# Rows scattered whole into per-expert regions and read back by one plain DMA, with a finer routing plan

## The chip, the cores and the metric

The kernel runs on one core of a Trainium2 chip. The metric is the device time of one execution in microseconds (us). The engines are PE (TensorE, matmuls), DVE (VectorE), ACT (ScalarE), POOL (GpSimd) and SP (SyncE, here only a queue that issues DMAs).

## What is computed

A gated linear attention (hgrn2) over 4 batches, 8 heads, 768 positions and a head size of 48 gives 3072 rows of 384 values; a noisy top-2 router sends each row to 2 of 8 experts, a feed-forward of 384 to 1024 to 384 each, and the two results are added with softmax gates.

```python
for t in range(S):                                  # S = 768, B = 4, H = 8, D = 48
    state = f[:, :, t, :, None] * state + einsum('bhd,bhe->bhde', k[:, :, t], v[:, :, t])
    y[:, :, t] = einsum('bhd,bhde->bhe', q[:, :, t], state)
x = y.transpose(0, 2, 1, 3).reshape(B * S, H * D)   # 3072 rows of 384
noisy_logits = x @ w_gate + log1p(exp(x @ w_noise)) * noise
top2, top2_w = two largest of 8, their softmax
for e in range(8):
    for k in range(2):
        mask = top2[:, k] == e
        h = maximum(x[mask] @ w1[e], 0.0)           # 384 to 1024
        out[mask] += top2_w[mask, k, None] * (h @ w2[e])   # 1024 to 384
```

## The kernel before

**Attention.** Time is cut into 6 chunks of 128 positions. A unit of work is (chunk c, batch b), 24 in all. Two units run at once, their instructions interleaved step by step (two `stream`s): here such two units are called a pair, so there are 12 pairs, 0 to 11, two for each chunk. `prep` (L245) of a unit makes its decayed q and k two units ahead: transposes on PE (L254), a sigmoid on ACT, products and reciprocals on DVE. `main` (L287) makes near scores (L304), four levels of scores for distances 8, 16, 32 and 64 (`sc`, L326), each with masked copies into `scores` (DVE L341, the last level ACT L339) and decays of q and k between levels; the products named `aid` (L281, L307, L310, L330, L334) are on POOL for the first two chunks (`WIDE = 2`) and on DVE after. Then come `kx` (L349), the output `y` (L355, L360), the state `ds` (L371), and a transpose `xp` (L383) whose copy (L384) leaves the unit's 128 rows of 384 values in `xrow`.

**Routing.** After each chunk's four batches `route` (L390) makes logits (`lg`, L398), the top two, each row's gates, and by matmuls with ones and a triangle (`rk`, L424 to L429) each row's place in its expert's region; `ati` (L440) holds the places. The rows with their gates go from `xrow` into a DRAM table `xd` by four ACT DMAs (L446). POOL then issues eight indirect scatters (L452), one per batch and rank, each behind a short `memset` of `pause` (L451): they write *row numbers*, 4 bytes each, into `ids`, the table of expert regions. Last, `choose` (L463, on DVE) picks which full blocks of 128 rows may be worked on: `LIST[c]` of them, 9 after chunk 1, then 8, 8, 8, and 22 after the last chunk, 55 in all.

**Experts.** A block of 128 rows of one expert is loaded by `fetch_rows` (L501): SP reads the block's place from `row_no`, loads 128 row numbers (`places`, L504), and POOL gathers the rows from `xd` by them (`rows_in`, L509). The `places` load that comes next after a router waits for all eight of its scatters, whatever block it serves, since it is given those dependencies by hand:

```python
ins = nc.sync.dma_start(out=pl, in_=ids[bass.ds(at, C), :]).ins
for other in placed:
    tc.add_manual_dep(ins, other.name, ...)
placed.clear()
```

`fetch_weights` (L513) loads the expert's two matrices, 3.1 MB, by SP (L518) into one of two slots, unless that slot has this expert already. `block` (L547) transposes the rows (`bx`, L539), multiplies in two halves (`bh`, L562, 24 matmuls each, relu on ACT L565 into one buffer `h`), multiplies back (`by`, L573, 8 matmuls), scales by the gate (`yo`, ACT L577, two buffers) and has POOL add the 128 rows into the output by an indirect DMA (`out_dram<-yo`, L578), here called the accumulate. `bx` of the next block is issued ahead of `by` if its rows have been asked for. Rows are fetched three blocks ahead (four buffers), weights two.

**Order.** PE, like each engine, takes its instructions as they were issued. A block is six steps (`YIELDS = 6`); `fill` puts as many of them between the attention's steps as a goal asks for. No block runs before chunk 2; after its step 20 of 28 (its second pair) 5 blocks are spread to its end; chunks 3, 4, 5 end at 13, 21 and 29 blocks; the remaining 26, here called the tail, follow the last router.

## Time and profile before

| what | value |
|---|---|
| three runs | 1095.98, 1096.57, 1100.07 us; median 1096.57 |
| the profiled execution | 1099.49 us, span 1097.7 us |
| mean granted PE clock | 0.903 |
| busy, share of the span | PE 956.9 us (87%), PEld 776.4, DVE 413.9, ACT 241.0, POOL 276.6 |
| moved by DMA | 176.49 MB, mean 161 GB/s |

The span is from the first to the last instruction that the profiler saw in one execution; that execution's own time is 1.8 us longer. PEld is PE's loading of weights, which goes on beside its matmuls. The granted clock is the share of full TensorE speed that the chip allowed. A row of the timeline gives start, duration, engine, line, operation, output<-input, sizes, and in brackets the engine's idle time before it with what ended it. Pairs 0 and 1 end at 94.0 us of the span, pair 2 at 151.0, pair 3 at 185.0, pair 4 at 248.5 and pair 5, the end of chunk 2, at 336.4; the routers of chunks 2 to 5 begin at 336.4, 485.2, 634.7 and 774.8 us.

### The profile page before, as it was taken

What the parts mean: (1) busy time and instruction counts of PE and PEld (TensorE: products, weight loads), DVE (VectorE), ACT (ScalarE), POOL (GpSimd) and SP (SyncE); (2) the same over time, 40 slices, a digit from 0 to 9 for tenths busy, and PEclk for the clock granted to TensorE, in tenths of its full rate; (3) what the DMA queues carried; (4) which work ended last, traced back from release to release, by engine and by line L of the source; (5) the groups of instructions that cost most, each with busy time, mean ns of one, the idle gap of its engine ahead of it and who ended that gap; (6) DMA issues with size and microseconds to landing.
All of it is one profiled execution on the core that took longest, in us unless ns stands there. A gap on an engine that the chain in (4) does not pass through costs nothing. (4 is left out here: it accounts for less than half of the span.)

```text
span 1097.7 us, 18858 instructions
## 1 busy us (share of the span) xinstructions
PE 956.9 (87%) x7357; PEld 776.4 (71%) x7357; DVE 413.9 (38%) x1043; ACT 241.0 (22%) x494; POOL 276.6 (25%) x343
## 2 busy tenths in 40 slices
PE   3687587837999799999799997999949999999996
PEld 2566466726878577878578885787837878788775
DVE  5765565928314535527436364342300000000000
ACT  2233233112222222223113231212201111111111
POOL 2753541310113211203111141111312222222221
PEclk9887677566998899999899998999879999999999
DMA  9594214192762498663977665676738147153663
GB/s 139 133 317 73 29 31 59 32 286 44 222 197 59 133 251 259 141 192 98 302 230 227 202 177 194 209 245 203 216 122 267 31 128 249 28 148 101 187 199 73
DMA packets 188007, 176.49 MB, mean 161 GB/s; under 512 B 118272, under 2 KB 167585, under 8 KB 187920
## 3 DMA queue, kind: packets, MB, share of 16 engines
q1 hardware_dynamic: 71648, 132.49, 35.6%
q10 hardware_dynamic: 103296, 23.70, 13.1%
q0 software_dynamic: 12976, 19.12, 8.4%
q8 instruction: 58, 0.95, 0.4%
q14 instruction: 29, 0.24, 0.1%
HBM read 203.08 MB, written 25.30 MB: 208 GB/s over the span
## 5 line engine op out<-in xcount | busy, mean ns | idle before, releaser
L562 PEld LDWEIGHTS bh<-xT,w 128*128 128x128 f32 x2640 | 309.7, 194 | 19.5 <-issue 7.2
L562 PE MATMUL bh<-xT,w 128*128 128x128 f32 x2640 | 317.6, 278 | 4.4 <-issue 4.4
L573 PE MATMUL by<-w,h 128*128 128x384 f32 x880 | 310.1, 502 | 0.0
L573 PEld LDWEIGHTS by<-w,h 128*128 128x128 f32 x880 | 166.5, 197 | 103.4 <-issue 10.9
L578 POOL DMA_INDIRECT out_dram<-yo,places x55 | 88.2, 1603 | 333.4 <-ACT yo L577 331.6
L326 PE MATMUL sc<-fT,kQ 48*128 48x128 f32 (+1 forms) x1536 | 126.9, 314 | 32.6 <-DVE scores L341 10.9
L509 POOL DMA_INDIRECT rows_in<-xd,places x55 | 59.6, 1084 | 356.8 <-DMA places<-ids 198.2
L326 PEld LDWEIGHTS sc<-fT,kQ 48*128 48x128 f32 (+1 forms) x1536 | 107.3, 203 | 55.9 <-issue 18.3
L541 DVE COPY xT<-bx 128x384 f32<-128x384 f32 x55 | 30.6, 556 | 304.7 <-PE bx L539 304.5
L565 ACT ACTIVATE h<-bh 128x512 f32<-128x512 f32 x110 | 65.7, 597 | 238.6 <-PE bh L562 207.4
L577 ACT ACTIVATE yo<-by,gt 128x384 f32<-128x384 f32 x55 | 31.9, 580 | 250.8 <-PE by L573 243.1
L539 PE MATMUL bx<-ident,rows_in 128*128 128x128 f32 x165 | 29.4, 290 | 38.7 <-DMA rows_in<-xd,places 38.7
L452 POOL DMA_INDIRECT ids<-tokens,ati x48 | 48.6, 1013 | 50.9 <-DVE gt L443 43.3
L330 DVE TENSOR_TENSOR kQ<-kQ,T 128x256 f32<-128x256 f32 x60 | 25.3, 422 | 91.6 <-PE sc L326 88.5
L331 DVE TENSOR_TENSOR fT<-fT,T 128x256 f32<-128x256 f32 x96 | 41.5, 436 | 25.8 <-PE sc L326 17.5
L341 DVE COPY_PREDICATED scores<-masks,sc 128x512 f32<-128x512 uint8 x72 | 50.9, 707 | 0.0
L539 PEld LDWEIGHTS bx<-ident,rows_in 128*128 128x128 f32 x165 | 20.3, 148 | 40.9 <-issue 40.7
L363 DVE COPY yT<-y 48x512 f32<-48x512 f32 x16 | 11.1, 695 | 87.2 <-ACT yT L363 87.2
L355 PE MATMUL y<-scores,v 128*48 128x128 f32 x384 | 32.9, 326 | 12.5 <-ACT scores L339 12.5
L280 DVE RECIPROCAL back<-ahead 128x256 f32<-128x256 f32 x24 | 41.7, 1737 | 0.2
L282 DVE RECIPROCAL ahead<-back 128x256 f32<-128x256 f32 x24 | 41.5, 1727 | 0.0
L304 PE MATMUL near<-qT,kT 48*128 48x128 f32 x384 | 32.6, 321 | 7.1 <-DVE qT L283 7.1
(134 smaller groups left out, 810.3 us busy)
## 6 DMA issues: line engine op xcount, KB each, us to landing
w<-in_moe_w_dram SPq DMA_DIRECT2D x110, 1536.0 KB
xd<-zero SPq DMA_DIRECT2D x12, 392.0 KB
xd<-xrow ACTq DMA_DIRECT2D x24, 196.0 KB
f<-in_f_logit_dram ACTq DMA_DIRECT2D x24, 192.0 KB
q<-in_q_dram ACTq DMA_DIRECT2D x24, 192.0 KB
k<-in_k_dram ACTq DMA_DIRECT2D x24, 192.0 KB
v<-in_v_dram ACTq DMA_DIRECT2D x24, 192.0 KB
out_dram<-zero SPq DMA_DIRECT2D x12, 384.0 KB
```

The lines of the kernel that those rows point to most:

```text
L280: nc.vector.reciprocal(k8[:, :, 4:8], q8[:, :, 4:8])
L282: nc.vector.reciprocal(q8[:, :, 0:4], k8[:, :, 0:4])
L326: nc.tensor.matmul(sc[0:nj, par * HP + hp, :], lhsT=kQ[rows(par), hp * C:hp * C + nj], rhs=qP[rows(par), cols(hp)], start=True, stop=True)
L331: nc.vector.tensor_tensor(qv, qv, Tv[:, :, 0:1].broadcast_to((128, x, m)), ALU.mult)
L341: nc.vector.copy_predicated(Av, masks[:, l].rearrange("j (x m) -> j x m", m=m).unsqueeze(1).broadcast_to((C, H, nb, m)), scv)
L452: ins = nc.gpsimd.indirect_dma_start(out=ids, out_offset=bass.IndirectOffsetOnAxis(ap=ati[:, r, b:b + 1], axis=0), in_=tokens[:, c, b:b + ...
L509: nc.gpsimd.indirect_dma_start(out=xr, out_offset=None, in_=xd, in_offset=bass.IndirectOffsetOnAxis(ap=pl.bitcast(U32), axis=0), bounds_ch ...
L539: nc.tensor.transpose(p[:, j * 128:(j + 1) * 128], xr[:, j * 128:(j + 1) * 128], ident)
L562: nc.tensor.matmul(hp[:, f * 128:(f + 1) * 128], lhsT=w1[:, j, fo * 128:(fo + 1) * 128], rhs=xT[:, j * 128:(j + 1) * 128], start=(j == 0), ...
L565: nc.scalar.activation(h[:, half * 4:half * 4 + 4, :].rearrange("p f t -> p (f t)"), hp, AF.Relu)
L573: nc.tensor.matmul(yp, lhsT=h[:, fo, :], rhs=w2[:, fo, :], start=(fo == 0), stop=(fo == FO - 1))
L578: nc.gpsimd.indirect_dma_start(out=out, out_offset=bass.IndirectOffsetOnAxis(ap=pl, axis=0), in_=yo, in_offset=None, bounds_check=N - 1, o ...
```

## The change

**Whole rows are scattered.** A row is now 393 words: 384 values, 8 gates and its own number. `xd` and `ids` give way to one table `xs` with a region for each expert and one block of free rows (gate 0, a number out of range). `route` writes gates and number into `xrow` (POOL copies the number, after-line L435), and POOL's eight indirect scatters (after-line L471) write the rows to their places. A block's rows come by one plain SP DMA, `rows_in<-xs` (after-line L524); POOL's gather and the ACT DMAs into `xd` are gone. That DMA waits for scatters by the tracked overlap on `xs`, from which the scatters of routers later than the block's own list are excluded. After the last router eight plain POOL DMAs (after-lines L479 to L481) write 128 free rows behind the end of each region, where a region's last block is not full.

**The plan is finer.** There are seven routers: after chunk 0 (four batches), after each half of chunk 1, then after each chunk. Their lists have 1, 4, 4, 8, 8, 8 and 22 blocks. Goals are now set by pair, in blocks done at the end of pairs 0 to 11: 0, 0, 1, 2, 4, 6, 10, 13, 17, 21, 24, 28; the other 27 are the tail. For the first two routers the scatters go one by one between POOL's other steps; for all, `choose` comes ahead of them on DVE.

**Smaller edits.** The twelve DMAs that cleared `xd` and the memsets of `rows_in` are gone; `out` is cleared by one DMA in pair 1. The first two `prep`s copy k and q, and ask for the next loads, right behind the sigmoid.

The diff, cut to its core (other functions only take the group `i` and its `nb` batches for the chunk and `B`):

```diff
-    R = N
+    R = N + C
     XG = DM
-    XW = DM + E
+    XI = DM + E
+    XW = DM + E + 1
     BIG = 1 << 20
-    LIST = [0, 9, 8, 8, 8, 22]
+
+    GROUPS = [(0, 0, 4), (1, 0, 2), (1, 2, 2), (2, 0, 4), (3, 0, 4), (4, 0, 4), (5, 0, 4)]
+    LIST = [1, 4, 4, 8, 8, 8, 22]
+
+    GOALS = [0, 0, 1, 2, 4, 6, 10, 13, 17, 21, 24, 28]
...
-    xd = dram.tile([N, XW], F32, tag="xd", name="xd")
-    ids = dram.tile([NID, 1], I32, tag="ids", name="ids")
+    xs = dram.tile([E * R + C, XW], F32, tag="xs", name="xs")
     rows_in = [ctile([XW], f"rows_in{i}") for i in range(NR)]
-    places = [ctile([1], f"places{i}", I32) for i in range(NR)]
...
-        for t in rows_in + [zero, counts, used]:
+        for t in (zero, counts, used, free):
             nc.gpsimd.memset(t, 0.0)
+        nc.gpsimd.memset(free.bitcast(I32)[:, XI:XW], BIG)
         nc.gpsimd.memset(experts, -1.0)
-        nc.gpsimd.memset(free, BIG)
-        nc.sync.dma_start(out=ids.rearrange("(p r) o -> p (r o)", p=128), in_=free)
-        clear(xd, XW)
-
-    def clear(t, w):
-        for i in range(N // 128 // ZR):
-            nc.sync.dma_start(out=t[i * ZR * 128:(i + 1) * ZR * 128].rearrange("(p r) d -> p (r d)", p=128),
-                              in_=zero[:, 0:ZR * w])
+        nc.sync.dma_start(out=xs[E * R:E * R + C], in_=free)
+
+    def clear():
+        nc.sync.dma_start(out=out.rearrange("(l p) d -> p l d", p=128),
+                          in_=zero.unsqueeze(1).broadcast_to((128, N // 128, DM)))
...
-    def prep(c, b):
+    def prep(c, b, first=False):
...
+        def rest():
+            nc.scalar.copy(kT, transposed("k"))
+            nc.scalar.copy(qT, transposed("q"))
+            load(c * B + b + B)
+
         nc.scalar.activation(fT, transposed("f"), AF.Sigmoid)
+        if first:
+            rest()
...
-    def route(c):
+    def route(i):
+        c, b0, nb = GROUPS[i]
...
+        yTc, xr = yT[c % 2], xrow[c][:, b0:b0 + nb, :]
...
+        nc.gpsimd.tensor_copy(xr.bitcast(I32)[:, :, XI:XW], tokens[:, c, b0:b0 + nb].unsqueeze(2))
+        yield
...
+        nc.vector.tensor_tensor(xr[:, :, XG:XG + E], gt2[:, 0], gt2[:, 1], ALU.add)
...
-        nc.vector.tensor_tensor(counts, counts, rk[:, B], ALU.add)
-        nc.vector.tensor_tensor(base, base, rk[:, B], ALU.add)
-        nc.vector.tensor_tensor(gt2, hot, wide(ex), ALU.mult)
-        nc.vector.tensor_tensor(xrow[c][:, :, XG:XG + E], gt2[:, 0], gt2[:, 1], ALU.add)
-        for b in range(B):
-            nc.scalar.dma_start(out=xd[b * S + c * C:b * S + (c + 1) * C, :], in_=xrow[c][:, b, :])
+        nc.vector.tensor_tensor(base, base, rk[:, nb], ALU.add)
+        nc.vector.tensor_tensor(counts, counts, rk[:, nb], ALU.add)
+        if i == NG - 1:
+            nc.vector.tensor_copy(tails, base)
+        choose(i)
 
         mine = []
-        for b in range(B):
+
+        def put(ins):
+            for other in mine:
+                tc.declare_no_dep(ins, other, reason="distinct places")
+            mine.append(ins)
+            placed.append((i, ins))
+
+        for b in range(nb):
             for r in range(2):
                 nc.gpsimd.memset(pause, 0.0)
-                ins = nc.gpsimd.indirect_dma_start(
-                    out=ids, out_offset=bass.IndirectOffsetOnAxis(ap=ati[:, r, b:b + 1], axis=0),
-                    in_=tokens[:, c, b:b + 1], in_offset=None).ins
-                for other in mine:
-                    tc.declare_no_dep(ins, other, reason="distinct places")
-                mine.append(ins)
-        placed.extend(mine)
-        if LIST[c]:
-            choose(c)
-            ready[0] += LIST[c]
+                put(nc.gpsimd.indirect_dma_start(
+                    out=xs, out_offset=bass.IndirectOffsetOnAxis(ap=ati[:, r, b:b + 1], axis=0),
+                    in_=xr[:, b, :], in_offset=None).ins)
+                if i < 2:
+                    yield
+        if i == NG - 1:
+
+            for e in range(E):
+                at = nc.gpsimd.value_load(tails[0:1, e:e + 1], min_val=0, max_val=E * R)
+                nc.gpsimd.memset(pause, 0.0)
+                put(nc.gpsimd.dma_start(out=xs[bass.ds(at, C), :], in_=free).ins)
+        ready[0] += LIST[i]
...
-        nc.vector.tensor_scalar_mul(row_no[:, g:g + L], row, float(C))
+        nc.vector.tensor_scalar(row_no[:, g:g + L], row, float(C), float(E * R), ALU.mult, ALU.min)
...
-        xr, pl = rows_in[g % NR], places[g % NR]
-        at = nc.sync.value_load(row_no[0:1, g:g + 1], min_val=0, max_val=NID - C)
-        ins = nc.sync.dma_start(out=pl, in_=ids[bass.ds(at, C), :]).ins
-        for other in placed:
-            tc.add_manual_dep(ins, other.name, mybir.DependencyInfo(mybir.DependencyClass.Sync,
-                                                                    mybir.DependencyReason.DATA), reason="all places")
-        placed.clear()
-        nc.gpsimd.indirect_dma_start(
-            out=xr, out_offset=None, in_=xd,
-            in_offset=bass.IndirectOffsetOnAxis(ap=pl.bitcast(U32), axis=0), bounds_check=N - 1, oob_is_err=False)
+        at = nc.sync.value_load(row_no[0:1, g:g + 1], min_val=0, max_val=E * R)
+        ins = nc.sync.dma_start(out=rows_in[g % NR], in_=xs[bass.ds(at, C), :]).ins
+
+        for i, other in placed:
+            if i > listed[g][0]:
+                tc.declare_no_dep(ins, other, reason="distinct places")
...
-        pl = places[g % NR].bitcast(U32)
+        ids = rows_in[g % NR].bitcast(U32)[:, XI:XW]
...
-    def stream(c, first):
-
-        for b in (first, first + 2):
-            n = c * B + b + 2
-            p = prep(*order[n]) if n < len(order) else iter(())
-            for i, _ in enumerate(main(c, b)):
-                if i in (1, 3):
-                    next(p, None)
-                yield
-
-    TURNS = B * (len(LEVELS) + 3)
+    def stream(n):
+
+        p = prep(*order[n + 2]) if n + 2 < len(order) else iter(())
+        for i, _ in enumerate(main(*order[n])):
+            if i in (1, 3):
+                next(p, None)
+            yield
+
+    TURNS = 2 * (len(LEVELS) + 3)
...
+            for _ in prep(*order[n], first=True):
...
-        for c in range(NCH):
-            xrow[c] = wk.tile([128, B, XW], F32, tag="xrow", name=f"xrow{c}", bufs=2)
-
-            first = 20 if c == WIDE else 0
-            start = done[0]
-            goal = YIELDS * max(0, sum(LIST[:c]) - KEEP)
+        for pair in range(len(order) // 2):
+            if pair % 2 == 0:
+                c = pair // 2
+                xrow[c] = wk.tile([128, B, XW], F32, tag="xrow", name=f"xrow{c}", bufs=2)
+            start, goal = done[0], YIELDS * GOALS[pair]
             t = 0
-            streams = [stream(c, 0), stream(c, 1)]
+            streams = [stream(2 * pair), stream(2 * pair + 1)]
             while streams:
                 for x in list(streams):
                     turn()
...
                         streams.remove(x)
                         continue
                     t += 1
-                    if c >= WIDE:
-                        fill(start + (goal - start) * max(0, t - first) // (TURNS - first))
-                if c == 0 and t == 4:
+                    fill(start + (goal - start) * t // TURNS)
+                if t == 4 and pair == 0:
                     later_constants()
-                if c == 1 and t == 4:
-                    clear(out, DM)
-            assert router is None
-            router = route(c)
-        while router:
+                if t == 4 and pair == 1:
+                    clear()
+            c, b0, nb = GROUPS[group]
+            if c * B + b0 + nb == 2 * pair + 2:
+                routers.append(route(group))
+                group += 1
```

**Where it moves instructions.** In these rows `places_157` to `places_160` and `rows_in_153` to `rows_in_156` are the four buffers in turn, `DMASW..` is a lane of POOL's DMAs, `DMAHW..` one of SP's and ACT's, and `w_0`, `w_1` are the two weight slots.

SP's queue before, from the row load of block 6 (first row) to that of block 8 (last row), both of the list made after chunk 1:

```order
L504 DMA places_159<-ids 128x1 [waits DMAHW1_49,DMASW7_49,DMASW2_49]
L514 TENSOR_LOAD load_no
...
L518 DMA w_0_161<-in_moe_w_dram 128x3x1024 [waits DMAHW2_49,PE_49]
...
L503 TENSOR_LOAD row_no
L503 ISA x2
L504 REGISTER_ALU
L504 DMA places_160<-ids 128x1 [waits DMASW5_49,DMASW4_49,DMASW6_49,DMASW3_49,DMASW7_49,DMASW2_49,DMAHW0_49,DMASW1_49,DMASW0_49]
...
L518 DMA w_1_162<-in_moe_w_dram 128x3x1024 [waits DMAHW6_49,DMAHW1_49,PE_49]
...
L504 DMA places_157<-ids 128x1 [waits DMAHW3_49]
```

The `places` load of block 7 stands behind all eight POOL lanes, that is behind every scatter of chunk 2, and the weights of the next block stand behind it.

SP's queue in the change, from the row load of block 7 (first row) to that of block 9 (last row), the first block of the list made after chunk 2:

```order
L524 DMA rows_in_156<-xs 128x393 [waits DMAHW3_49,DMAHW7_49,DMASW3_49,DVE_49]
L531 TENSOR_LOAD load_no
...
L535 DMA w_1_158<-in_moe_w_dram 128x3x1024 [waits DMAHW6_49,DMAHW0_49,PE_49]
...
L524 DMA rows_in_153<-xs 128x393 [waits DMAHW0_49,DMASW4_49,DVE_49]
...
L535 DMA w_0_157<-in_moe_w_dram 128x3x1024 [waits DMAHW4_49,DMAHW1_49,PE_49]
...
L523 TENSOR_LOAD row_no [waits DVE_49]
L523 ISA x2
L524 ISA
L524 DMA rows_in_154<-xs 128x393 [waits DMAHW3_49,DMASW5_49,DMAHW5_49,DMASW4_49,DVE_49]
```

Blocks 7 and 8 wait on one POOL lane each, that of the accumulate that read their buffer's row numbers; block 9 waits on two, the accumulate's and that of the eighth scatter.

PE in pair 2 (chunk 1, batches 0 and 1) before, from the last level's scores on:

```order
L326 MATMUL sc_1_0_1200<-fT_0_661,kQ_0_951 64x128 x8
L326 MATMUL sc_1_1_1214<-fT_1_696,kQ_1_1009 64x128 x8
L349 MATMUL kx_0_1228<-ident,kQ_0_951 128x128 x4
L355 MATMUL y_0_1234<-scores_113,v_0_596 48x128 x8
L360 MATMUL y_0_1234<-fT_0_661,st_0_588 48x128 x8
```

The same place in the change:

```order
L334 MATMUL sc_1_0_1197<-fT_0_646,kQ_0_944 64x128 x8
L334 MATMUL sc_1_1_1211<-fT_1_681,kQ_1_1004 64x128 x8
L556 MATMUL bx_1246<-ident,rows_in_153 128x128 x3
L579 MATMUL bh_0_1257<-xT_1250,w_0_157 128x128 x12
L579 MATMUL bh_0_1271<-xT_1250,w_0_157 128x128 x6
L357 MATMUL kx_0_1278<-ident,kQ_0_944 128x128 x4
L363 MATMUL y_0_1284<-scores_113,v_0_581 48x128 x8
```

Block 0 is now between the scores and `kx`: the attention behind it on PE goes on when block 0's rows and the weights of its first halves are there.

POOL after the last chunk, before:

```order
L578 DMA out_dram<-yo_6676,places_157 3072x384
L451 MEMSET pause 128x1
L452 DMA ids<-tokens,ati_6696 27392x1
...
L509 DMA rows_in_156<-xd,places_160 128x392
L578 DMA out_dram<-yo_6822,places_158 3072x384
```

And in the change, down to the accumulate of block 27 (last row):

```order
L435 COPY xrow_5427<-tokens 128x4
L470 MEMSET pause 128x1
L471 DMA xs<-xrow_5427,ati_6567 25728x393
...
L479 TENSOR_LOAD tails
L479 ISA x2
L480 MEMSET pause 128x1
L481 ISA
L481 DMA xs<-free 128x393
...
L595 DMA out_dram<-yo_6710,rows_in_156 3072x384
```

Where the gather and the accumulate followed eight scatters, one accumulate now follows eight scatters and eight writes of free rows, each with its register load and memset.

## Rows read from the trace of the kernel before

**Rows 1.** The page: busy time, share of the span and instructions of each engine.

```profile
PE 956.9 (87%) x7357; PEld 776.4 (71%) x7357; DVE 413.9 (38%) x1043; ACT 241.0 (22%) x494; POOL 276.6 (25%) x343
```

**Rows 2.** Stretches: us, busy PE, PEld, DVE, ACT, POOL; PE clock, DMA share, GB/s.

```profile
94.00:151.00 57.00, 40.43 (x342) 35.06 (x340) 26.52 (x61) 14.42 (x32) 26.80 (x42) 0.61 0.23 43
151.00:185.00 34.00, 27.18 (x299) 22.45 (x298) 23.60 (x38) 11.45 (x26) 8.67 (x17) 0.80 0.34 48
185.00:248.50 63.50, 40.18 (x343) 34.47 (x342) 35.91 (x104) 13.40 (x30) 12.55 (x18) 0.60 0.54 146
248.50:336.40 87.90, 81.13 (x627) 67.20 (x627) 35.02 (x82) 19.02 (x39) 10.59 (x8) 0.88 0.55 150
336.40:774.80 438.40, 416.12 (x3413) 333.10 (x3412) 203.72 (x539) 104.12 (x214) 92.69 (x96) 0.96 0.66 199
774.80:1097.70 322.90, 295.29 (x1792) 237.26 (x1790) 27.19 (x118) 50.02 (x85) 77.67 (x68) 0.96 0.48 142
```

**Rows 3.** Timeline of PE: the waits for rows after each router.

```profile
380.40 0.88 PE L539 MATMUL bx<-ident,rows_in 128*128 128x128 f32 x3 [6.42 <-DMA rows_in<-xd,places]
...
529.12 0.87 PE L539 MATMUL bx<-ident,rows_in 128*128 128x128 f32 x3 [7.95 <-DMA rows_in<-xd,places]
...
677.10 0.87 PE L539 MATMUL bx<-ident,rows_in 128*128 128x128 f32 x3 [7.15 <-DMA rows_in<-xd,places]
...
820.22 0.87 PE L539 MATMUL bx<-ident,rows_in 128*128 128x128 f32 x3 [16.08 <-DMA rows_in<-xd,places]
820.88 7.06 PE L573 MATMUL by<-w,h 128*128 128x384 f32 x16
```

**Rows 4.** Timeline of POOL: scatters after chunk 2 (first) and chunk 5 (first, eighth).

```profile
350.00 1.00 POOL L452 DMA_INDIRECT ids<-tokens,ati  x1 [0.19 <-DVE whole L474]
...
786.84 0.97 POOL L452 DMA_INDIRECT ids<-tokens,ati  x1 [3.12 <-DVE gt L443]
...
795.70 0.95 POOL L452 DMA_INDIRECT ids<-tokens,ati  x1 [0.19 <-issue]
```

**Rows 5.** Timeline of SP's queue: the first `places` load after those scatters.

```profile
370.86 0.34 SPq L504 DMA_DIRECT2D places<-ids  x1
...
811.12 0.35 SPq L504 DMA_DIRECT2D places<-ids  x1
```

**Rows 6.** Timeline of PE: one block of the tail.

```profile
849.47 5.52 PE L562 MATMUL bh<-xT,w 128*128 128x128 f32 x48
854.83 0.49 PE L539 MATMUL bx<-ident,rows_in 128*128 128x128 f32 x3
855.15 5.33 PE L573 MATMUL by<-w,h 128*128 128x384 f32 x16
860.32 5.52 PE L562 MATMUL bh<-xT,w 128*128 128x128 f32 x48
```

**Rows 7.** Timeline of PE: idle gaps in pairs 2 and 4.

```profile
118.40 2.08 PE L326 MATMUL sc<-fT,kQ 48*128 48x128 f32 x16 [8.54 <-POOL fT L307]
...
226.02 1.08 PE L349 MATMUL kx<-ident,kQ 128*128 128x128 f32 x4 [4.36 <-DVE kQ L330]
239.29 1.95 PE L355 MATMUL y<-scores,v 128*48 128x128 f32 x16 [12.19 <-ACT scores L339]
```

**Rows 8.** Timeline of SP's and ACT's queues: first weights, and loads held behind them.

```profile
222.10 1.16 SPq L518 DMA_DIRECT2D w<-in_moe_w_dram  x2
...
229.64 0.37 ACTq L220 DMA_DIRECT2D f<-in_f_logit_dram  x1
234.49 0.37 ACTq L220 DMA_DIRECT2D q<-in_q_dram  x1
```

**Rows 9.** Timeline of POOL: an accumulate and the gather that waited for it.

```profile
393.19 1.76 POOL L578 DMA_INDIRECT out_dram<-yo,places  x1 [4.43 <-ACT yo L577]
401.32 1.05 POOL L509 DMA_INDIRECT rows_in<-xd,places  x1 [6.37 <-DMA out_dram<-yo,places]
```

**Rows 10.** Timeline of DVE: its first work after the last router.

```profile
821.12 0.56 DVE L541 COPY xT<-bx 128x384 f32<-128x384 f32 x1 [26.64 <-PE bx L539]
```

More of the change, by code (lines that the diff above doesn't have):

```diff
@@ L81 @@
     NR = 4
-    KEEP = 4
     WIDE = 2
     assert (H * D, 2 * LEVELS[-1], B * S, FO, B) == (DM, C, N, 8, 4)
-    assert all(sum(LIST[:c + 1]) <= max(0, 2 * B * (c + 1) - E + 1) for c in range(NCH - 1))
+    assert all(sum(LIST[:i + 1]) <= 2 * sum(nb for _, _, nb in GROUPS[:i + 1]) - E + 1 for i in range(NG - 1))
     assert NB == 2 * N // C + E - 1
@@ L148 @@
     base = ctile([E], "base")
-    i_no = {L: ctile([L], f"i_no{L}") for L in sorted(set(LIST)) if L}
+    i_no = {L: ctile([L], f"i_no{L}") for L in sorted(set(LIST))}
     tokens = ctile([NCH, B], "tokens", I32)
@@ L166 @@
     row_no = ctile([NB], "row_no", I32)
-    picks = [ctile([LIST[c], E], f"picks{c}") if LIST[c] else None for c in range(NCH)]
-    ZR = 2
-    zero = ctile([ZR * XW], "zero")
-    free = ctile([NID // 128], "free", I32)
+    picks = [ctile([LIST[i], E], f"picks{i}") for i in range(NG)]
+    zero = ctile([DM], "zero")
+    free = ctile([XW], "free")
+    tails = ctile([E], "tails", I32)
     def iota(t, pattern, mult, first=0):
@@ L276, in prep @@
         yield
-        nc.scalar.copy(kT, transposed("k"))
-        nc.scalar.copy(qT, transposed("q"))
-        load(c * B + b + B)
+        if not first:
+            rest()
         nc.vector.reciprocal(k8[:, :, 4:8], q8[:, :, 4:8])
@@ new lines, in route @@
+        nc.tensor.matmul(rk[:, 1:nb + 1], lhsT=ones, rhs=chosen[:, 0:1].broadcast_to((128, nb, E)), start=True,
+                         stop=False, skip_group_check=True)
+        nc.tensor.matmul(rk[:, 0], lhsT=before, rhs=chosen[:, 0], start=False, stop=True, skip_group_check=True)
+        nc.tensor.matmul(rk[:, 1:nb], lhsT=before, rhs=chosen[:, 1:nb], start=False, stop=False, skip_group_check=True)
+        for b in range(1, nb):
+            nc.tensor.matmul(rk[:, b + 1:nb + 1], lhsT=ones, rhs=chosen[:, b:b + 1].broadcast_to((128, nb - b, E)),
+                             start=False, stop=(b == nb - 1), skip_group_check=True)
@@ L518, in fetch_weights @@
             nc.sync.dma_start(out=w, in_=src, bounds_check="skip_entire_dma", cond=go)
-    listed = [(c, i) for c in range(NCH) for i in range(LIST[c])]
+    listed = [(c, i) for c in range(NG) for i in range(LIST[c])]
     ready, rows_done, weights_done = [0], [0], [0]
@@ L578, in block @@
         nc.gpsimd.indirect_dma_start(
-            out=out, out_offset=bass.IndirectOffsetOnAxis(ap=pl, axis=0), in_=yo, in_offset=None,
+            out=out, out_offset=bass.IndirectOffsetOnAxis(ap=ids, axis=0), in_=yo, in_offset=None,
             bounds_check=N - 1, oob_is_err=False, compute_op=ALU.add)
@@ L616 @@
         for n in range(2):
-            for _ in prep(*order[n]):
+            for _ in prep(*order[n], first=True):
                 pass
-        router = None
+        routers = []
+        group = 0
         def turn():
-            nonlocal router
-            if router and next(router, True):
-                router = None
-        for c in range(NCH):
-            xrow[c] = wk.tile([128, B, XW], F32, tag="xrow", name=f"xrow{c}", bufs=2)
-            first = 20 if c == WIDE else 0
-            start = done[0]
-            goal = YIELDS * max(0, sum(LIST[:c]) - KEEP)
+            if routers and next(routers[0], True):
+                routers.pop(0)
+        for pair in range(len(order) // 2):
[3 more added lines that the diff above has]
+            start, goal = done[0], YIELDS * GOALS[pair]
             t = 0
-            streams = [stream(c, 0), stream(c, 1)]
+            streams = [stream(2 * pair), stream(2 * pair + 1)]
             while streams:
```

54 lines of the change are left out of this document (24 added, 30 removed).

## The prediction

> **What bounds the kernel now.** I read the page first, then the busy time by stretch, then the PE timeline's idle gaps, then the queues that end them.
>
> The page: PE is busy 956.9 us of the 1097.7, so 140.8 us are idle [rows 1]. By stretch [rows 2]: from 336.4 us (end of chunk 2) to the end PE is busy 416.1 + 295.3 of 761.3 us at a granted clock of 0.96, almost PE-bound; from 94.0 to 248.5 us (pairs 2, 3, 4) it is busy 107.8 of 154.5 us at 0.60 to 0.80, a chain of DVE, POOL, ACT and small matmuls with no expert block beside it; 248.5 to 336.4 us holds the first 4.75 blocks.
>
> So time can come from two places: PE's gaps in the PE-bound part, and filling the early part with blocks. In the PE-bound part the gaps are few and named: 6.42, 7.95, 7.15 and 16.08 us before a `bx`, all ended by the rows' DMA [rows 3]. What is late there: after a router POOL issues eight scatters of row numbers, the first at 350.00 us [rows 4], and SP's next `places` load goes out only at 370.86 us [rows 5], when all eight have landed, 20.9 us after the first issue; after the last router 786.84 to 811.12 us, 24.3 us. The rows that PE waits for at 380.40 us are those of block 7, which is in the *old* list; the order (section on the change) shows its `places` load held by eight POOL lanes although only blocks from 9 on need the new scatters.
>
> **The change, part by part.** The sum is made against the profiled execution, span 1097.7 us. A block in the tail costs 10.85 us of PE, from one bh to the next (849.47 to 860.32 us) [rows 6].
>
> *1. Old lists no longer wait (336.4 to 774.8 us).* Row loads are plain SP DMAs, and in the order block 7's row load waits only for its buffer. Only block 9 and on waits for the new scatters, and block 9 is needed in the middle of block 8, some 45 us after the router starts (2.5 blocks at a quarter of a 68 us pair each, plus the router's own matmuls); landed scatters: about 34 us after it (336.4 to 370.86). So 6.42 + 7.95 + 7.15 = 21.5 us go. Behind such a gap PE runs cold: bx 0.87 for 0.49 and by 7.06 for 5.33 us [rows 3, 6], 2.1 us each, 6.3 more. Gain 27.8, bounds 15 (if block 9 is late by one such gap of half size at each router) and 27.8. The goals also do 22 blocks here for 24: -21.7 us of work. 438.4 - 27.8 - 21.7 = 388.9.
>
> *2. The tail (774.8 us to the end).* It has 27 blocks, not 26: +10.85. Five listed blocks are left at the last router, not four, and none waits for scatters, so the 16.08 us wait on rows goes. What is late next: POOL now issues eight row scatters, then eight plain DMAs for the tails, each behind a register load and a memset, and only then block 27's accumulate into out. ACT's `yo` of block 29 needs that buffer (two buffers), and block 30's h stands behind it on ACT. The eight scatters are issued by 795.70 + 0.96 = 796.7 us, 1.27 us apart [rows 4]. A tail write is unknown: 1.27 us like a scatter below, 3.0 above (the 24.3 us in which eight landed, by eight). I take 2.2, for the register load comes on top of a scatter's issue: the accumulate goes out at 814 us, takes 1.6 and lands 6.4 us later (393.19 + 1.76 to 401.32) [rows 9], 822; a queue still landing scatters until 811 pushes it to about 826. PE gets to block 30's by near 815 us and needs two ACT steps after the landing: wait about 12 us, bounds 0 and 25 (seventeen landings at 3.0). 322.9 + 10.85 - (16.1 - 12) = 329.7.
>
> Here one rule bears. DVE has nothing to do for 26.64 us before 821.12 us [rows 10], yet these are the slowest eight scatters of the run, 24.3 us against 20.9 beside a busy DVE [rows 4, 5]. The Trainium skill (SBUF — State Buffer, "SBUF: two separate sides") says that DMAs issued from GpSimd starve for descriptors while DVE holds the shared port; by that rule the tail, with DVE idle, would land at once and the sum would be 12 us lower. The trace disagrees, and the row decides.
>
> *3. Pairs 2 and 3 (94.0 to 185.0 us).* Today 57.0 + 34.0 = 91.0 us [rows 2]. Removed: the second stream's POOL steps no longer stand behind all eight scatters, 8.54 us of PE [rows 7]; the scatters now go one by one between POOL's steps, 1.27 us each [rows 4], covered by cold matmuls (if not covered, 10 us come back). Added: 1.75 blocks, 19.0 us. And two waits: PE's block 0 stands behind the last level's matmuls, and its rows need the eighth scatter, then SP loads rows, then weights. A landing of 2.6 us (20.9 by eight) and 7.5 us from the weights' issue to the end of their first half (222.10 to 229.64) [rows 8] make 10; bounds 5 and 20. Block 1 waits in pair 3 for its four scatters with block 0's accumulate between them: 7 us, bounds 0 and 12.4 (both halves, to 234.49) [rows 8]. 91.0 - 8.5 + 19.0 + 17 = 118.5.
>
> *4. Pairs 4 and 5 (185.0 to 336.4 us).* Today 151.4 us with 4.75 blocks. ACT stood at its loads' issue until the first weights had landed (229.64 and 234.49 us, [rows 8]), which left PE idle 4.36 + 12.19 us [rows 7]; the first weights come two pairs earlier, so this moves into term 3. Four blocks are left here. Above: 151.4 - 16.6 - 0.75 x 10.85 = 126.7. Below: as full as the later pairs, (438.4 - 27.8 - 24 x 10.85)/6 = 25.0 us of attention, (25.0 + 21.7) x 2 = 93.4. Pair 5's own attention beside its blocks, 87.9 - 4.75 x 10.85 = 36.4 [rows 2], lies between; I take the middle, 110.
>
> *5. Edits at nothing.* The 12 DMAs that cleared xd, the four 0.4 us memsets of rows_in and the POOL gathers (1.06 us each) go, `choose` moves ahead of the scatters on DVE, the first two preps copy k and q before the small copies: all beside the startup's loads or a PE that is the bound; if the cover is gone, 1 or 2 us either way.
>
> Sum: 94.0 + 118.5 + 110 + 388.9 + 329.7 = 1041.1 us of span. The profiled execution took 1.8 us more than its span and 2.9 us more than the median of the three runs (1099.49 to 1096.57), so **1040 us** as such a median, 5.2% less. The mechanism's own range: 12 and 16.7 us in the early part, 12 at the tail, up to 13 at the routers: 1015 to 1070.
>
> **Rivals.**
> *A, slower: scatters of whole rows land one by one.* Today's scatters carry 4 bytes a row; an accumulate, which carries whole rows, lands 6.4 us after its issue [rows 9]. If each row scatter occupies the queue that long, eight take 51 us. Block 9 is then 22 us late and the two later lists 6 each; pair 2 waits 24 more, pair 3 19, the tail (17 landings) 70: 147 us, 1187. It turns slower than before where it costs more than 57 us, at some 4.3 us a landing. Against it: the gathers of whole rows are issued at a scatter's price and PE's steady tail lives with one gather and one accumulate per block.
> *B, the early blocks are not hidden.* Waits of 20 and 12.4 us and pairs 4 and 5 at 126.7: 32 us more, 1072. For it: PE takes instructions in order, so a late row load holds the attention chain too; and ACT's loads share semaphores with SP's, which is what held it at 221 us today.
> *C, everything fits.* Waits of 5 and 0, pairs 4 and 5 at 93.4, no wait in the tail: 41 us less, 999. For it: from 336.4 us on pairs with four blocks do run full [rows 2].
> *D, the change doesn't do what it says:* old lists still wait, through another lane. Term 1's 27.8 us stay: 1068. Against it stands the order.
>
> **How the numbers follow.** Forecast 0.63, A 0.07, B 0.14, C 0.11, D 0.05. About half a per cent, 5.5 us, is what a measurement of this kernel tells from no change. Only A, or B beyond its bounds, comes near the old time: slower 0.06, same 0.03, faster 0.91. The range leaves out A, part of C and the top of B: 1008 to 1072.
>
> **What would show it.** Right: no `bx` after 350 us waits for its rows; SP issues the row loads of a list's last blocks before the newest scatters land; PE's wait in the tail is on ACT's h or yo, ended by an accumulate's landing; two waits of 5 to 20 us at the first two blocks; the end of chunk 2 near 322 us, with one block more done. Wrong: gaps of 6 us or more after each router still ended by the rows' DMA (D or A), a span from 94 to the end of chunk 2 over 260 us (B), or scatters that take more than 4 us each from the first issue to the last landing (A).

## The result and the profile after

The change takes 1040.8 us (median of 4 runs) beside 1098.2 us for the kernel before: 0.948 of its time, 95% interval 0.944 to 0.952. The forecast was 1040. The profiled execution took 1043.8 us, span 1042.2 us, mean granted clock 0.936.

Busy time by stretch, columns as in [rows 2]; the stretches are the start (pairs 0 and 1), pair 2, pair 3, pair 4, pair 5, the rest to the last router, and the tail:

```profile
0.00:102.54 102.54, 61.36 (x553) 51.74 (x554) 62.65 (x102) 28.62 (x68) 46.54 (x94) 0.90 0.68 119
102.54:171.38 68.84, 46.61 (x401) 40.71 (x400) 38.27 (x82) 16.31 (x35) 23.30 (x41) 0.68 0.38 102
171.38:229.91 58.53, 43.75 (x381) 37.13 (x379) 32.18 (x78) 15.19 (x34) 15.76 (x29) 0.74 0.55 160
229.91:282.00 52.09, 48.55 (x426) 38.74 (x424) 36.71 (x104) 16.40 (x35) 7.48 (x9) 0.90 0.63 179
282.00:329.48 47.48, 46.67 (x464) 37.83 (x463) 32.06 (x69) 14.12 (x31) 3.33 (x4) 1.00 0.72 188
329.48:722.11 392.63, 389.49 (x3281) 314.50 (x3280) 200.47 (x533) 99.29 (x208) 62.40 (x73) 0.98 0.72 217
722.11:1042.20 320.09, 307.04 (x1871) 245.50 (x1869) 28.82 (x125) 52.31 (x89) 57.21 (x59) 0.98 0.55 168
```

| term of the sum | forecast | measured | off by |
|---|---|---|---|
| start | 94.0 | 102.5 | +8.5 |
| pairs 2, 3 (term 3) | 118.5 | 127.4 | +8.9 |
| pairs 4, 5 (term 4) | 110 | 99.6 | -10.4 |
| to the last router (term 1) | 388.9 | 392.6 | +3.7 |
| tail (term 2) | 329.7 | 320.1 | -9.6 |
| span | 1041.1 | 1042.2 | +1.1 |

Every term is off by 4 to 10 us and the sum by 1: that the errors cancel is luck, so the experiments go to the terms.

**Start.** Timeline of PE and of ACT with its DMA queue, end of pair 0:

```profile
65.77 1.95 PE L363 MATMUL y<-scores,v 128*48 128x128 f32 x16 [6.87 <-ACT scores L347]
```

```profile
52.11 3.53 ACTq L221 DMA_DIRECT2D k<-in_k_dram  x1
55.68 0.59 ACT L265 COPY kT<-kp 128x512 f32<-128x512 f32 x1 [5.26 <-PE sc L334]
55.73 5.24 ACTq L221 DMA_DIRECT2D f<-in_f_logit_dram  x1
...
61.01 3.14 ACTq L221 DMA_DIRECT2D q<-in_q_dram  x1
...
65.14 1.06 ACT L347 COPY scores<-sc 64x512 f32<-64x512 f32 x2 [8.38 <-issue]
```

ACT stands 3 to 5 us at the issue of single loads, it copies the scores only after 8.38 us without other work, and PE's `y` waits for that. SP issued the one DMA that clears the output, 4.6 MB, at 47.05 us.

**The first two blocks.** Timeline of PE in pairs 2 and 3:

```profile
147.72 0.87 PE L556 MATMUL bx<-ident,rows_in 128*128 128x128 f32 x3 [7.52 <-DMA rows_in<-xs]
153.45 6.54 PE L579 MATMUL bh<-xT,w 128*128 128x128 f32 x36 [4.86 <-DMA w<-in_moe_w_dram]
...
177.07 0.58 PE L440 MATMUL rk<-chosen,ones 128*128 128x16 f32 x2 [2.74 <-DVE dx L432]
...
194.45 2.08 PE L334 MATMUL sc<-fT,kQ 48*128 48x128 f32 x16 [3.97 <-POOL kQ L338]
199.84 0.90 PE L556 MATMUL bx<-ident,rows_in 128*128 128x128 f32 x3 [3.31 <-DMA rows_in<-xs]
...
218.56 1.08 PE L363 MATMUL y<-scores,v 128*48 128x128 f32 x16 [3.80 <-ACT scores L347]
```

Block 0 waits 12.4 us for rows and weights (10 forecast), block 1 3.3 us (7 forecast). The other three waits are not in the sum: `rk` is the added half router's, `sc` waits for POOL, where block 0's accumulate stands between that router's scatters, and `y` waits for ACT, which stood at the issue of its loads again:

```profile
210.94 5.01 ACTq L221 DMA_DIRECT2D f<-in_f_logit_dram  x1
```

**After the routers** of chunks 2 to 4 no `bx` waits; PE idles 3.1 us in 392.6. In the tail the sixteen DMAs stand ahead of one accumulate. Timelines of POOL, of SP's queue and then of PE:

```profile
734.83 1.00 POOL L471 DMA_INDIRECT xs<-xrow,ati  x1 [16.11 <-DVE have L497]
...
744.81 0.60 POOL L481 DMA_DIRECT2D xs<-free  x1
...
753.85 0.54 POOL L481 DMA_DIRECT2D xs<-free  x1 [0.51 <-issue]
754.69 1.65 POOL L595 DMA_INDIRECT out_dram<-yo,rows_in  x1 [0.30 <-issue]
```

```profile
761.86 0.35 SPq L524 DMA_DIRECT2D rows_in<-xs  x1
```

```profile
764.41 0.52 PE L556 MATMUL bx<-ident,rows_in 128*128 128x128 f32 x3 [1.39 <-DMA rows_in<-xs]
...
771.02 5.60 PE L579 MATMUL bh<-xT,w 128*128 128x128 f32 x48 [0.94 <-DMA w<-in_moe_w_dram]
776.86 0.52 PE L556 MATMUL bx<-ident,rows_in 128*128 128x128 f32 x3 [0.24 <-DMA rows_in<-xs]
```

PE loses 2.6 us, where [rows 3] had 16.08.

### The profile page after: what moved, and what is told of

Its sections match the earlier page's. It is cut to its first block, busy times and chain, and to the rows that moved or that the text cites. A ratio compares the mean times of both kernels' runs of the same rounds, so it can differ in the third digit from the quotient of the medians.

```text
span 1042.2 us, 18705 instructions
## 1 busy us (share of the span) xinstructions
PE 943.5 (91%) x7361; PEld 766.2 (74%) x7361; DVE 431.2 (41%) x1093; ACT 242.2 (23%) x500; POOL 216.0 (21%) x309
## 5 line engine op out<-in xcount | busy, mean ns | idle before, releaser
L579 PEld LDWEIGHTS bh<-xT,w 128*128 128x128 f32 x2640 | 309.3, 194 | 25.6 <-issue 10.5
L590 PE MATMUL by<-w,h 128*128 128x384 f32 x880 | 305.0, 498 | 0.0
L595 POOL DMA_INDIRECT out_dram<-yo,rows_in x55 | 86.3, 1569 | 577.2 <-ACT yo L594 524.9
L334 PE MATMUL sc<-fT,kQ 48*128 48x128 f32 (+1 forms) x1536 | 123.9, 308 | 17.6 <-POOL kQ L338 5.9
L334 PEld LDWEIGHTS sc<-fT,kQ 48*128 48x128 f32 (+1 forms) x1536 | 104.7, 198 | 39.6 <-issue 19.2
L471 POOL DMA_INDIRECT xs<-xrow,ati x48 | 48.4, 1009 | 163.6 <-issue 82.0
L339 DVE TENSOR_TENSOR fT<-fT,T 128x256 f32<-128x256 f32 x96 | 47.3, 497 | 17.3 <-PE sc L334 9.9
L363 PE MATMUL y<-scores,v 128*48 128x128 f32 x384 | 29.1, 300 | 10.7 <-ACT scores L347 10.7
L312 PEld LDWEIGHTS near<-qT,kT 48*128 48x128 f32 x384 | 28.9, 227 | 12.4 <-issue 7.1
L319 DVE COPY_PREDICATED scores<-near,near 128x1024 f32<-128x1024 uint8 x24 | 31.0, 1294 | 16.1 <-PE near L312 16.1
```

What stands on the lines that cost most here:

```text
L312: nc.tensor.matmul(sc[:, par, cols(hp)], lhsT=kM[rows(par), cols(hp)], rhs=qM[rows(par), cols(hp)], start=True, stop=True)
L334: nc.tensor.matmul(sc[0:nj, par * HP + hp, :], lhsT=kQ[rows(par), hp * C:hp * C + nj], rhs=qP[rows(par), cols(hp)], start=True, stop=True)
L339: nc.vector.tensor_tensor(qv, qv, Tv[:, :, 0:1].broadcast_to((128, x, m)), ALU.mult)
L471: put(nc.gpsimd.indirect_dma_start(out=xs, out_offset=bass.IndirectOffsetOnAxis(ap=ati[:, r, b:b + 1], axis=0), in_=xr[:, b, :], in_offset ...
L579: nc.tensor.matmul(hp[:, f * 128:(f + 1) * 128], lhsT=w1[:, j, fo * 128:(fo + 1) * 128], rhs=xT[:, j * 128:(j + 1) * 128], start=(j == 0), ...
L590: nc.tensor.matmul(yp, lhsT=h[:, fo, :], rhs=w2[:, fo, :], start=(fo == 0), stop=(fo == FO - 1))
```

## The experiments

The runs came from three chips, on which the kernel before took 1108.2 (e1 to e4), 1104.4 (e5 to e8) and 1107.1 us (e9 to e12). Times are compared within one chip, except where the text names the other. Line numbers shift by up to 20.

**e1: the old rule put back in the change.** The next row load behind a router waits for all its scatters:

```diff
         for i, other in placed:
-            if i > listed[g][0]:
+            if i > 2:
+                tc.add_manual_dep(ins, other.name, ...)
+            elif i > listed[g][0]:
                 tc.declare_no_dep(ins, other, reason="distinct places")
+        placed[:] = [x for x in placed if x[0] <= 2]
```

> The change with one rule of the kernel before put back: the first row load asked for after a router waits for all eight of its scatters (after the last router, for the tails too), so the loads of blocks 8, 15, 23 and 30, all of old lists, wait again. The theory of the prediction (term 1): PE waits for rows after each of three routers come back, 6 to 8 us each with 2 us of cold matmuls behind them, and one of some 12 us after the last: 30 to 36 us more than the change's 1040.8, 1070 to 1077. Rival: the plan is now one block further ahead and the row scatters land 7 us after their issue, so at the first three routers the wait is covered and only the last shows: 1041 to 1053.

Measured: 1066.3 us, 0.957 of before (0.950 to 0.965). On the same chip e2 and e4, which have the change's goals from here on and not the rule, take 414.6 and 414.4 us from chunk 2's end to the last router; e1:

```profile
330.40:745.23 414.83, 401.63 (x3281) 323.09 (x3280) 201.25 (x533) 99.89 (x208) 62.11 (x73) 0.95 0.69 205
745.23:1068.50 323.27, 307.33 (x1871) 245.02 (x1869) 28.82 (x125) 52.38 (x89) 57.20 (x59) 0.98 0.55 167
```

The rule costs nothing at three routers and 2.8 us in the tail (323.3 for e2's 320.4). The rival holds, though its time does not: with the rule (e1) or without it (e2, e4), these runs take 22 us longer than the change between chunk 2's end and the last router (414.8 for 392.6 in e1). Of these 10 us are idle time of PE and 12 slower work, at a granted clock of 0.95 for 0.98; the last section shows the rows that go with them.

**e3: the old plan on the new way of the rows.**

```diff
-    GROUPS = [(0, 0, 4), (1, 0, 2), (1, 2, 2), (2, 0, 4), (3, 0, 4), (4, 0, 4), (5, 0, 4)]
-    LIST = [1, 4, 4, 8, 8, 8, 22]
+    GROUPS = [(0, 0, 4), (1, 0, 4), (2, 0, 4), (3, 0, 4), (4, 0, 4), (5, 0, 4)]
+    LIST = [1, 8, 8, 8, 8, 22]
-    GOALS = [0, 0, 1, 2, 4, 6, 10, 13, 17, 21, 24, 28]
+    GOALS = [0, 0, 0, 0, 0, 5, 9, 13, 17, 21, 25, 29]
...
-            if i > listed[g][0]:
+            if i > max(listed[g][0], 1):
```

> The new way of the rows with about the old plan: one router a chunk, lists of 1, 8, 8, 8, 8 and 22 blocks, no block before pair 5, goals 5, 9, 13, 17, 21, 25, 29. Theory of the prediction's sum: the way of the rows alone gains terms 1 and 2 (27.8 us of waits, some 14 us at the tail) and pair 2's 8.5 us, and loses the 8 us of the start: about 42 us under the kernel before, 1056, and the plan gives the other 15. Rival: the gain is the plan's, blocks in the idle early pairs: then this one stays within 20 us of the kernel before, over 1078.

Measured: 1062.2 us, 0.958 (0.952 to 0.965): a larger gain than the theory gave this part, and no more than e1's or e4's time on that chip. The way of the rows carries all of the gain that can be told there; the plan adds none. One caution: from chunk 2's end to the last router e3 takes 427.5 us for 413.9 in e6, the same blocks on another chip: 13.6 us longer, where e1 is 22 longer than the change. So this chip may count against the new plan.

**e6: the old plan and the old rule together**, e3 with e1's rule.

> The old plan on the new way of the rows, and now with the old rule too: the first row load after a router waits for all eight scatters, here blocks 7, 15, 23 and 31. If the rule itself made the waits after the routers (the prediction's term 1), PE's gaps of 6 to 8 us before a bx come back at three routers and one of 10 to 16 us in the tail: 30 us more than the old plan without the rule, 0.985 of the kernel before. Rival: what made those waits was the rule together with the two steps of the rows (numbers, then a gather) and scatters that landed 11 to 14 us after the last issue; with one plain load and landings of 7 us the rule costs under 3 us a router: 0.96 to 0.97.

Measured: 1055.5 us, 0.954 (0.948 to 0.959). Stretches from chunk 2's end, then POOL's last scatter and SP's queue at the first router, then PE there and in the tail:

```profile
324.33:738.25 413.92, 413.92 (x3414) 333.19 (x3412) 203.73 (x539) 103.97 (x214) 65.54 (x75) 0.98 0.71 217
738.25:1055.20 316.95, 295.81 (x1792) 236.35 (x1790) 27.58 (x119) 50.05 (x85) 55.59 (x59) 0.96 0.51 157
```

```profile
347.24 1.06 POOL L471 DMA_INDIRECT xs<-xrow,ati  x1 [0.19 <-issue]
```

```profile
350.67 0.35 SPq L524 DMA_DIRECT2D rows_in<-xs  x1
```

```profile
361.77 0.49 PE L560 MATMUL bx<-ident,rows_in 128*128 128x128 f32 x3
...
776.01 0.87 PE L560 MATMUL bx<-ident,rows_in 128*128 128x128 f32 x3 [10.55 <-DMA rows_in<-xs]
```

Here the waiting load is block 7's as in the kernel before, and still PE never idles before the last router: 413.9 us for the same 24 blocks that took 438.4 [rows 2]. The load goes out 2.4 us after the last scatter's issue (348.3 to 350.67). The eighth scatter of the kernel before:

```profile
359.01 1.06 POOL L452 DMA_INDIRECT ids<-tokens,ati  x1 [0.19 <-issue]
```

There the load went out 10.8 us after that issue (360.07 to 370.86), and from there a second step, the gather, took 9.5 us more until `bx` (370.86 to 380.40) [rows 3, 5]. A row load in the new way takes some 2.5 us until `bx` (in the change's tail 761.86 to 764.41). So what ended the waits is a chain some 15 us shorter (20.3 to 4.9), not the rule. The slack at this router fits: PE runs the same work up to that `bx` in both kernels and is ready for it 13.9 us after the eighth scatter's issue before (380.40 less the wait of 6.42) and 13.5 us after it in e6 (361.77). A chain of 20.3 us overruns that by the 6.4 us that PE waited, one of 4.9 does not. By the same numbers, as an estimate, either half alone would just have fitted: 10.8 and 2.5, or 2.4 and 9.5; neither was run.

In the tail, where the rule holds the load behind the tails too, 10.55 us are lost, and the `by` behind them takes 7.92 us for 5.33. Together that is the 13.1 us by which e6 is longer than e5, the change on the same chip, so the plan adds nothing that can be told there either. The time is below both expectations, 0.985 and 0.96 to 0.97.

**e2: the output cleared in 12 pieces.**

```diff
-        nc.sync.dma_start(out=out.rearrange("(l p) d -> p l d", p=128),
-                          in_=zero.unsqueeze(1).broadcast_to((128, N // 128, DM)))
+        for i in range(12):
+            nc.sync.dma_start(out=out[i * 256:(i + 1) * 256].rearrange("(l p) d -> p l d", p=128),
+                              in_=zero.unsqueeze(1).broadcast_to((128, 2, DM)))
```

> The change with the output cleared by 12 DMAs of 256 rows, as before, and not by one of 4.6 MB. Theory: that one DMA is what held ACT at the issue of its loads in pair 0 (3.5 and 5.2 us for single issues, scores copied 8.4 us late); with pieces the end of pair 0 comes back from 72.3 to about 66 us and the whole is 6 to 7 us shorter: 1034. Rival: ACT is held by its own loads, since the first preps ask for them earlier; then pair 0 stays at 72 us and the time at 1041.

Measured: 1055.1 us, 0.949 (0.943 to 0.955), 11 us less than e1 on its chip, 3 of which are e1's tail. The router of chunk 0 starts at 94.76 us for e1's 102.53. ACT in pair 0:

```profile
51.92 2.20 ACTq L222 DMA_DIRECT2D k<-in_k_dram  x1
...
54.21 1.39 ACTq L222 DMA_DIRECT2D f<-in_f_logit_dram  x1
...
58.56 1.06 ACT L348 COPY scores<-sc 64x512 f32<-64x512 f32 x2 [3.32 <-DVE fT L340]
```

The one large DMA was the cause: 7.8 us between these two profiles. In e5, the change once more, the same router starts at 98.81 us, so single executions differ by some 4 us here; the issues of 3.5 and 5.3 us are in it too. What holds ACT in pair 3, where no clear runs (5.01 us above), was not tested. The Trainium skill (DMA: Bandwidth & Descriptors, "Issuing engines are not separate DMA queues") says that DMAs run on the same 16 DMA engines whichever engine starts them. These rows agree, SP's clear holds ACT's loads; but the section calls the time to initiate a DMA usually small beside the DMA itself, and here the issue of one load took 5.24 us.

**e4: one router for chunk 1.** GROUPS and LIST as in e3, GOALS 0, 0, 1, 1, 4, 6 and on as in the change.

> The change with one router for chunk 1 instead of two halves: lists 1, 8, 8, 8, 8, 22 and goals 0, 0, 1, 1, 4, 6, 10 and on as in the change, so that one block moves from pair 3 to pair 4. Theory: the extra half router is what made pair 3 longer than forecast (58.5 us): without it and its block pair 3 takes 36 to 40 us, pair 4 some 12 us more than its 52 for the block and the larger router: 8 to 10 us less in all, 1031 to 1033. Rival: pair 4's three blocks come late behind their scatters, rows and weights, and the time is the change's or up to 10 us longer.

Measured: 1065.0 us, 0.958 (0.952 to 0.964).

```profile
101.73:203.06 101.33, 73.95 (x697) 63.69 (x696) 63.44 (x120) 27.43 (x60) 33.70 (x59) 0.71 0.34 81
203.06:329.80 126.74, 110.10 (x966) 90.64 (x965) 70.52 (x182) 32.02 (x69) 17.39 (x23) 0.88 0.65 183
```

Pairs 2 and 3 are 26 us shorter than in the change, pairs 4 and 5 27 us longer; the moved block, 10.85 us, is in both. The theory falls: what the half router and its block cost in pair 3 is paid in pair 4 instead.

**e5: the change again**, beside e6 to e8.

> The change itself, beside the next three on one chip, so that their times can be held against its own and not only against the kernel before. Every theory expects 0.94 to 0.955 of the kernel before; its stretches (start, pairs 2 to 5, from there to the last router, tail) are the yardstick.

Measured: 1042.4 us (1035.3 to 1044.3), 0.942 (0.937 to 0.948).

**e7: the work behind the last scatters doubled.**

```diff
                 put(nc.gpsimd.dma_start(out=xs[bass.ds(at, C), :], in_=free).ins)
+                nc.gpsimd.value_load(tails[0:1, e:e + 1], min_val=0, max_val=E * R)
+                nc.gpsimd.memset(pause, 0.0)
+                nc.gpsimd.dma_start(out=spare[e], in_=free)
```

> The change with twice the work on POOL after the last router: behind each of the eight tail writes the same write once more, with its register load and memset, into a table that nothing reads. In the change eight tails took 9.6 us of POOL and PE lost 2.6 us behind them. Theory (term 2's mechanism, only over-sized): block 27's accumulate goes out 9.6 us later, its landing releases block 29's yo later, and PE waits 8 to 10 us more in the tail, about 10 us more than the change. Rival: PE's loss there comes from rows and weights that SP loads late, and POOL has slack: under 3 us more.

Measured: 1047.0 us, 0.946 (0.941 to 0.952), 4.6 us more than e5, half of the 10 expected; the tail takes 323.8 us for e5's 318.8. POOL, ACT, SP's queue, PE:

```profile
746.58 0.60 POOL L482 DMA_DIRECT2D xs<-free  x1
...
766.93 1.65 POOL L599 DMA_INDIRECT out_dram<-yo,rows_in  x1 [0.30 <-issue]
```

```profile
771.54 0.58 ACT L598 ACTIVATE yo<-by,gt 128x384 f32<-128x384 f32 x1 [16.96 <-DMA out_dram<-yo,rows_in]
```

```profile
771.56 0.34 SPq L528 DMA_DIRECT2D rows_in<-xs  x1
```

```profile
774.09 0.88 PE L560 MATMUL bx<-ident,rows_in 128*128 128x128 f32 x3 [9.29 <-DMA rows_in<-xs]
```

The accumulate goes out 20.3 us after the first tail write (746.58 to 766.93) and not 9.9, and PE's one wait is 9.29 us, where e5 has 1.42 and 1.56. So the mechanism of term 2 holds, with little slack left; but the accumulate's landing lets two things go at once, ACT's `yo` and the row load of block 31, which reuses block 27's buffer, and it is the rows that PE waits for last.

**e8: a version that beats the change**: e2's clear, the preps in the old order, and loads asked for a step later:

```diff
-            load(c * B + b + B)
...
         yield
+        load(c * B + b + B)
...
-            if i in (1, 3):
+            if i in (1, 3, 5):
...
-            for _ in prep(*order[n], first=True):
+            for _ in prep(*order[n]):
```

> A version that may beat the change: the output is cleared by 12 DMAs, the first two preps run in the old order, and every prep asks for its next loads one step later, behind the copy of the last level's scores on ACT. Theory: the start gives back 8 us and 1 us, and PE's 4 us in pair 3 behind scores, ended by ACT's issue of loads, go: 11 to 13 us less than the change. Rival: the loads asked for later arrive late or the stall moves to the next copy on ACT: 8 to 9 us less, the start's alone.

Measured: 1030.7 us (1029.6 to 1031.4) beside e5's 1042.4: 11.8 us less; 0.932 of before (0.927 to 0.937). No `y` waits on ACT's scores in pair 0 or pair 3. How the 11.8 us divide is not settled, since e5's profiled execution was its shortest, 1035.3 us.

**e11, e12: e8 again, and with the last router's scatters and tails apart.** In e12 each of the last router's scatters and tail writes is followed by a `yield`.

> The version with the cleared output in pieces, the old order of the first preps and later loads once more, beside the next one on one chip: 0.932 of the kernel before, give or take 0.006.

> That version, and after the last router one scatter or one tail write for each step of the blocks instead of sixteen in a row, so that block 27's accumulate goes out ahead of most of them. Theory: what PE lost in the tail (2.6 us in the change, 9.3 when POOL had twice the work) hung on that accumulate's landing; it goes to nothing, 2 to 4 us less than the run beside it. Rival: the new rows' scatters now end some 25 us later and a new wait takes its place: no gain, or some us longer.

Measured: 1054.97 and 1054.99 us, 0.955 (0.948 to 0.961) and 0.953 (0.946 to 0.959). On this chip e8 stands nearer to the kernel before; the last section has what differs there. Spreading brings nothing that can be told: the tail stretch is 320.1 for 321.4 us. It had little to remove, since in e11's profile no `bx` waits in the tail.

**e9, e10: scatters of row numbers beside those of rows.** To e6, from chunk 2 on, eight extra scatters behind the eight, and the row load waits for them. They write 4 bytes a row in e9 and 512 in e10, where the source is `xr[:, b, 0:128]`:

```diff
+                    put(nc.gpsimd.indirect_dma_start(
+                        out=extra, out_offset=bass.IndirectOffsetOnAxis(ap=ati[:, r, b:b + 1], axis=0),
+                        in_=tokens[:, c, b0 + b:b0 + b + 1], in_offset=None).ins)
```

> The old plan and old rule of the run before (e6), and behind the eight row scatters of each router from chunk 2 on also eight scatters of the row numbers alone, 4 bytes a row as in the kernel before, into a table that nothing reads; the first row load after a router now waits for these. There the row load went out 2.4 us after the last row scatter was issued; in the kernel before the same load went out 10.8 us after the last scatter of numbers. Theory: small scatters themselves land late, so the load goes out 9 to 14 us after the last issue, and PE's gaps of 5 us or more before a bx come back after three routers. Rival: they land like whole rows, 3 us, and what was late in the kernel before was something else there, its gather or its DMAs of the rows: then only POOL's ten more microseconds show.

> As the run before this one, but each row of the extra scatters is 512 bytes (128 words of the row) and not 4. Theory: it is the size of the rows written, so these land like whole rows and the load goes out 2.4 to 3 us after the last issue. Rival: it is the number of scatters in flight, sixteen for eight: then it goes out as late as with 4 bytes.

Measured: 1107.6 and 1107.5 us, one execution each. The load goes out 5.4 us after the last issue with 4 bytes (358.8 to 364.18) and 2.4 us with 512 (360.5 to 362.9). POOL's last scatter and SP's row load, e9 and then e10:

```profile
357.86 0.96 POOL L482 DMA_INDIRECT extra<-tokens,ati  x1 [0.19 <-issue]
364.18 0.36 SPq L534 DMA_DIRECT2D rows_in<-xs  x1
```

```profile
359.58 0.96 POOL L482 DMA_INDIRECT extra<-xrow,ati  x1 [0.19 <-issue]
362.91 0.01 SPq L534 DMA_DIRECT2D rows_in<-xs  x1
```

No `bx` waits for rows behind the first three routers, where the expectation of e9 had gaps of 5 us or more. The 5.4 us lie between the theory's 9 to 14 and the rival's 3: small rows do land later, but by 3 us and not by the 8 that part the kernel before from e6; what makes up the rest is open. The Trainium skill (DMA: Bandwidth & Descriptors, "Specifications") has transfers under 512 bytes done as read-modify-write; the order of these two runs agrees, from one execution each. That both stand at the time of the kernel before came from elsewhere. PE in e9, during the scatters:

```profile
347.32 0.27 PE L335 MATMUL sc<-fT,kQ 48*128 48x128 f32 x1 [1.08 <-issue]
348.06 0.27 PE L335 MATMUL sc<-fT,kQ 48*128 48x128 f32 x1 [0.47 <-issue]
348.79 0.36 PE L335 MATMUL sc<-fT,kQ 48*128 48x128 f32 x1 [0.46 <-issue]
```

## Why the prediction was right, point by point

*Term 1, old lists no longer wait: size right, reason wrong.* 27.8 us were to go; in e6, with the same 24 blocks but on another chip, 24.5 went (438.4 to 413.9). But the step "only block 9 and on waits for the new scatters" is not what did it: with the rule back (e1, e6) PE waits at none of the three routers. The waits ended because rows came by one load, 2.4 us behind the scatters, instead of a load and a gather, the first 10.8 us behind them, against a slack of some 13.5 us. I read the rule from the order and its price from the gap, and never compared the load's lateness with the slack of a shorter chain. That the size came out is luck. Rival D is thereby moot: its 27.8 us would not have been lost.

*Term 2, the tail: mechanism right, size wrong.* The block costs its 10.85 and the 16.08 us go. The waits behind block 27's accumulate are there but 2.6 us and not 12: 322.9 + 10.85 - 16.1 + 2.6 = 320.3, measured 320.1. The mis-sized step is "I take 2.2" for a tail write; it is 1.24 (9.9 us by eight, 744.81 to 754.69), about the lower bound. e7 shows the 9.29 us that a price of twice that brings. The path was half right: the waits are ended by rows and weights from block 31 on, not by ACT's `h` or `yo`. I took from the Trainium skill (SBUF — State Buffer, "SBUF: two separate sides") that scatters beside an idle DVE would land at once. The section says only what keeps GpSimd from writing descriptors while DVE runs some of its operations, so that step was mine, and it fails: the median landing of the scatters is 7.4 us in the tail, with DVE busy for 5.1 of 27.2 us (734.8 to 762.0), 5.5 to 7.3 us at the routers of chunks 2 to 4 with a busier DVE, and 2.7 us in pair 2 with DVE busy for 28.2 of 29.8 us (115.2 to 145.0). The DMAs moved 94 GB/s in the last of these stretches and 307 in the tail's, which goes with the landings; whether it is the cause was not tried.

*Terms 3 and 4: 228.5 forecast, 227.0 measured, 8.9 and 10.4 us off against each other.* Waits at blocks 0 and 1 were 15.7 us for 17. Left out of term 3 were three waits, 2.74 us in the added half router, 3.97 us behind block 0's accumulate on POOL, and 3.80 us behind ACT's loads: 10.5 us together. Pairs 4 and 5 fill nearly to the lower bound of 93.4, so "I take the middle" was the wrong end. What I credited to the early blocks is worth little: e3, without them, needs 224.6 us for pairs 2 to 5 (101.6 to 326.2) with one block fewer, and in the whole takes no longer than e1 and e4 on its chip.

*Term 5, edits at nothing: wrong.* Its list has the 12 dropped DMAs into `xd` and leaves out that the 12 that clear the output became one of 4.6 MB. That one cost 7.8 us (e2), since it filled the way of ACT's loads. The cover that I named, the startup's loads, was the victim. Copying k and q first held the first reciprocal 1.1 us, within the "1 or 2 us": in e8, with the old order, the first `near` starts at 25.20 us for e5's 26.11.

*Rivals.* A is out: scatters of whole rows are issued 1.27 us apart and overlap in landing. B is out, pairs 2 to 5 took 227 us. C's nearly full pairs 4 and 5 came, its 999 us did not: pairs 2 and 3 took 127.4 us for its 106.5, the start 8.5 more than the sum had.

*Signs.* No `bx` behind the routers of chunks 2 to 4 waited, and SP issued a row load at 347.12 us, between the scatters of 343.4 and 352.6. Missed were the tail, where two `bx` wait for rows (1.39 and 0.24 us), block 1's wait, below 5 us, and the end of chunk 2, at 329.5 us and not 322.

## What to carry to other kernels

A wait named by a dependence is not priced by that dependence: ask how late its last link is against the slack, and remove links before rules. An edit costed at nothing, or left off the list, needs the queue that it shares named, here that of the loads beside it. A forecast whose terms were 8 to 10 us off in four places and 1 us off in sum has to be checked term by term.
